# Fewer products for the size bounds, Strassen sums left in PSUM, and a small scaling on GpSimd

## The chip, the core and the metric

The kernel runs on one core of a Trainium2 chip. The metric is the device time of one execution in microseconds (us). The engines are TensorE (PE, with its weight loads listed as PEld), VectorE (DVE), ScalarE (ACT), GpSimd (POOL) and SyncE (SP), which only issues DMAs here. Each engine runs its own queue in order and waits for others by semaphores.

## The reference

Two attention layers over 2048 tokens, model width 1024, 32 heads of 32, written side by side in the output.

```
A: q, k, v = x@wq, x@wk, x@wv        # 4 segments of 512 tokens
   per segment s: a_dot = softmax(q k^T/sqrt(32) + mask) v
                  a_mem = phi(q) M / (phi(q) z + 1e-6)
                  o     = g*a_mem + (1-g)*a_dot;  M += phi(k)^T v;  z += sum phi(k)
   out_A = o @ wo
B: q, k, v = split(x @ wqkv);  pq = q@w_phi, pk = k@w_phi     # per head
   phi(t) = [softmax(t), softmax(-t)]
   o = phi(pq) (phi(pk)^T v) / (phi(pq) sum(phi(pk)) + 1e-6)
   out_B = o @ wo
```

## The kernel before

Every large product is computed in fp16 with each operand split into a high and a low half, so that one product is three matmuls. For the split, values are scaled by a bound of their size; the bounds are computed on the chip.

The work is described as operations with an engine, a duration, a priority, and the buffers read and written. A planner (`Graph.run`) then lays all of them in one order per engine by list scheduling with these durations, takes PSUM banks (8, by kinds `proj`, `s`, `misc`, `pv`, `kv`) as they come free in the plan, and keeps operations that are marked `port` on DVE apart from those of POOL. The code order therefore sets only priorities; a changed operation can change the order of everything after it.

*Layer A* (to about 900 us) is 32 units: for each half of the sequence (two segments), eight groups of four heads, two segments each. `produce` makes the queries, keys and values of a unit, `attend` the attention. Before a unit, `bounds(k, segs)` makes scale factors for queries and keys of group `k`, and `bounds_v(k, segs)` those for values. A bound is a sum over partitions of (column maxima of the segment, `xam`) times (column sums of the weights, `wgb`, `wvb`): the kernel multiplies them on PE, with one segment's `xam` column broadcast as the 128x128 fp32 weights and the group's `wgb` columns as the moving operand, one product for each segment and each group. Then DVE scales and inverts (tile `bd`, `bv`), and POOL makes the remaining factors. The weights of the groups for the second half (`k >= 8`, for values `k >= 4`) are the same ones as for the first half, loaded again.

*Layer B* (from about 870 us) takes 8 pairs of token blocks. A product of 256 tokens by all 1024 columns is done by `strassen`: seven products of 12 matmuls each, in three PSUM banks X, Y, Z, with results `(row half, column half)`. Some products serve two results: `keep` (ACT) copies a bank to an SBUF tile of tag `cs` (`pk` for the first value products), and `add` (DVE) adds another bank to it. Product 4 ends in X, is added to the kept one, and product 6 goes on accumulating in X. Each result goes to `out`: for values `vout` (split on ACT and DVE); for keys and queries `expo`, which on DVE takes the maximum and the minimum over each head's 32 columns (`mx`), subtracts (tile `e`), has ACT take exponentials, sums them on DVE (`r`), for keys scales `r` by 1/EUP, and inverts it. POOL then multiplies `e` by `r`. The keys and values of all pairs come first (about 950 to 1250 us), with their sum products in bank kind `kv`; then the queries with the output projection (to about 1600 us); last, the output product of layer A.

Of the kernel before, what the change touches and what calls it, by code (L numbers as in the profile page):

```python
# [255 lines left out]
def tile_kernel(ctx: ExitStack, tc: tile.TileContext, ax, aw, awv, awo, beta, bx, bwqk, bwv, bphi, bwo, out):  # L256
# [51 lines left out]
    big = const.tile([128, 6], F32, name="big")  # L308
    nc.vector.memset(big, 0.0)
    wsc = const.tile([128, 3, 2, 2], F32, name="wsc")  # L310
    osc2 = const.tile([128, 2, 2], F32, name="osc2")
# [257 lines left out]
    def strassen(x, w, prio, kinds, tag, out):  # L569
# [15 lines left out]

        def add(t, ps):
            op(DVE, 0.62, lambda: nc.vector.tensor_tensor(t(), t(), ps(), op=OP.add), r=[ps], w=[t], prio=prio)  # L587
# [91 lines left out]
    def bounds(k, segs, prio):  # L679


        bd = bds.get(k) or bds.setdefault(k, G.buf("a", [128, 5, 2, 2], F32, "bd", 4))
        s0, n, kk = segs[0], len(segs), k % NG
        v, w = slice(s0 % 2, s0 % 2 + n), [(bd, x % 2) for x in segs]
        ps = bank("misc", [128, 2, 2], "bounds")
        for x in segs:
            op(PE, 0.14, lambda x=x: nc.tensor.matmul(
                ps()[:, x % 2], xam[:, x:x + 1].to_broadcast([128, 128]), wgb[:, kk], start=True, stop=True),
               r=[(xams, x), (wgbs, (kk, 0)), (wgbs, (kk, 1))], w=[ps], prio=prio, need=[bd])
        op(DVE, 0.1, lambda: nc.vector.tensor_scalar(bd()[:, 3, v], ps()[:, v], 2.0 ** -12, 1e-30, op0=OP.mult, op1=OP.max),  # L690
           r=[ps], w=w, prio=prio)
        op(DVE, 0.12, lambda: nc.vector.reciprocal(bd()[:, 2, v], bd()[:, 3, v]), w=w, prio=prio)
        op(DVE, 0.1, lambda: nc.vector.scalar_tensor_tensor(
            bd()[:, 4, v, 0], bd()[:, 3, v, 0], SCALE, bd()[:, 3, v, 1], op0=OP.mult, op1=OP.mult), w=w, prio=prio)
        op(POOL, 0.2, lambda: nc.gpsimd.tensor_tensor(
            bd()[:, 0, v], xsc[:, s0:s0 + n, 0:1].to_broadcast([128, n, 2]), wgs[:, kk, :, 0][:, None, :].to_broadcast([128, n, 2]), op=OP.mult),
           r=[*((xscs, x) for x in segs), (wgss, (kk, 0)), (wgss, (kk, 1))], w=w, prio=prio)
        op(POOL, 0.2, lambda: nc.gpsimd.tensor_tensor(bd()[:, 2, v], bd()[:, 2, v], bd()[:, 0, v], op=OP.mult), w=w, prio=prio)
        op(POOL, 0.2, lambda: nc.gpsimd.tensor_scalar(bd()[:, 1, v], bd()[:, 0, v], -1.0, None, op0=OP.mult), w=w, prio=prio)

    def bounds_v(k, segs, prio):

        bv = bvs.get(k) or bvs.setdefault(k, G.buf("a", [128, 3, 2], F32, "bv", 3))
        s0, n, kk = segs[0], len(segs), k % 4
        v, w = slice(s0 % 2, s0 % 2 + n), [(bv, x % 2) for x in segs]
        ps = bank("misc", [128, 2], "bounds")
        for x in segs:
            op(PE, 0.14, lambda x=x: nc.tensor.matmul(
                ps()[:, x % 2:x % 2 + 1], xam[:, x:x + 1].to_broadcast([128, 128]), wvb[:, kk:kk + 1], start=True, stop=True),
               r=[(xams, x), (wvbs, kk)], w=[ps], prio=prio, need=[bv])  # L710
# [3 lines left out]
        a, b = s0 % 2, (s0 + n - 1) % 2  # L714
        op(DVE, 0.1, lambda: nc.vector.scalar_tensor_tensor(
            big[:, 0:1], bv()[:, 1, a:a + 1], bv()[:, 1, b:b + 1], big[:, 0:1], op0=OP.max, op1=OP.max), r=w, w=[(bigs, 0)], prio=prio)
        op(POOL, 0.4, lambda: nc.gpsimd.tensor_scalar(bv()[:, 0, v], xsc[:, s0:s0 + n, 0], wvs[:, kk, 0:1], None, op0=OP.mult),
           r=[*((xscs, x) for x in segs), (wvss, kk)], w=w, prio=prio)

    def values(u):  # L720

        s, g = units[u]
        k = group(u) // 2
        w, x, P, d = wt[k, "v"], xt[s], 2 * u, un[u]
        d["bv"] = bv = bvs[k]
        i2, n0, vf = s % 2, 128 * (g % 2), vfb[u % 3]
        sc = d["sc"] = G.buf("a", [128, 4], F32, "sc", 4)
        op(POOL, 0.39, lambda: nc.gpsimd.tensor_scalar(sc(), gate1[:, 4 * g:4 * g + 4], bv()[:, 1, i2:i2 + 1], None, op0=OP.mult),
           r=[gates, (bv, i2)], w=[sc], prio=P + VPRIO)
# [5 lines left out]
        op(ACT, 0.62, lambda: nc.scalar.activation(vf()[:, :, 0:128], ps(), AF.Copy, scale=bv()[:, 0, i2:i2 + 1]),  # L735
           r=[ps, (bv, i2)], w=[vf], prio=P + VPRIO)

    def produce(u):
# [10 lines left out]
        for m in (1, 0):  # L749
            ps = bank("proj", [128, 512])  # L750
            product((ps, ps), lambda a, c: (w, (m, a, c // 4), lambda m=m: w()[:, m, a, c, :]), at(x), NC, P, dur=0.215)
            E = P
            op(ACT, 0.57, lambda ps=ps, m=m: nc.scalar.activation(half(m, 0), ps(), AF.Copy, scale=bd()[:, 2, i2, m:m + 1]),
               r=[ps, (bd, i2)], w=[(h3, (m, 0))], prio=E)
            op(DVE, 0.6, lambda ps=ps, m=m: nc.vector.scalar_tensor_tensor(
                half(m, 1), ps(), bd()[:, 2, i2, m:m + 1], half(m, 0), op0=OP.mult, op1=OP.subtract),
               r=[ps, (h3, (m, 0)), (bd, i2)], w=[(h3, (m, 1))], prio=E)
# [4 lines left out]
            if (m == 1 and s < NSEG - 1) or (m == 0 and s > 0):  # L762
                d[name] = p = G.buf("a", [128, 512], F32, name, 2)
                z = G.buf("a", [128, 512], F32, "z", 1)
                for o, i in ((z, 0), (p, 1)):
                    op(ACT, 0.59, lambda o=o, i=i, ps=ps, m=m: nc.scalar.activation(o(), ps(), AF.Relu, scale=bd()[:, i, i2, m:m + 1]),
                       r=[ps, (bd, i2)], w=[o], prio=E)
# [4 lines left out]
    def attend(u):  # L772
        s, g = units[u]
        d, P = un.pop(u), 2 * u + 1
        st, vl, vf, bd, bv, i2 = stk[u % 3], vlb[u % 2], vfb[u % 3], bds[group(u)], d["bv"], s % 2
        KR, QR = [(st, (1, r)) for r in range(3)], [(st, (0, r)) for r in range(3)]
# [60 lines left out]
        def v4(t):  # L837
            return t()[:, :, 0:128].rearrange("p c (h d) -> p c h d", d=32)

        act(0.52, lambda: nc.scalar.activation(vl()[:, :, :, 33:65], v4(vf), AF.Copy, scale=bv()[:, 2, i2:i2 + 1]),  # L840
            r=[vf, (bv, i2)], w=[(vl, 0)])
        dve(0.6, lambda: nc.vector.scalar_tensor_tensor(
            vl()[:, :, :, 0:32], v4(vf), bv()[:, 2, i2:i2 + 1], vl()[:, :, :, 33:65], op0=OP.mult, op1=OP.subtract),
            r=[vf, (bv, i2), (vl, 0)], w=[(vl, 1)], port=True)
# [46 lines left out]
        def scores(blocks, diag):  # L891
# [13 lines left out]
            pe(0.218, f, r=KR + QR + [(st, (1, 3))] + [(st, (0, 3 + h)) for h, _ in blocks], w=[ps])  # L905
            act(0.59, lambda: nc.scalar.activation(ps(), ps(), AF.Exp, bias=0.0, scale=bd()[:, 4, i2, 0:1]), r=[(bd, i2)], w=[ps])  # L906
            ph = G.buf("a", [128, 2, 512], F16, "ph", 6)
# [234 lines left out]
    for u in range(NU):  # L1142
# [12 lines left out]
        if u % 4 == 1 and u // 4 + 1 < 8:  # L1155
            load_wv(u // 4 + 1, 2 * u + 0.5)
            if u // 4 + 1 < 4:
                keep_wv(u // 4 + 1)
            x = 2 * ((u // 4 + 1) // 4)
            bounds_v(u // 4 + 1, [x, x + 1], 2 * u + 0.5)  # L1160
        if u % 2 and k < NG:
            keep_wg(k, [(un[u]["h3"], (1, 1))])
        if u % 2 == 0 and k + 2 < NU // 2:
            load_wg(k + 2, 2 * u + 3.5)
            x = 2 * ((k + 2) // NG)
            bounds(k + 2, [x, x + 1], 2 * u + 3.5)
        attend(u)
# [11 lines left out]
    def expo(ps, prio, sk, up=None):  # L1179
# [23 lines left out]
        if up is not None:  # L1203
            op(DVE, 0.1, lambda: nc.vector.tensor_scalar(r(), r(), 1.0 / up, None, op0=OP.mult), r=[r], w=[r], prio=prio)
        op(DVE, 0.27, lambda: nc.vector.reciprocal(r(), r()), r=[r], w=[r], prio=prio)  # L1205
# [345 lines left out]
    for c in range(NT // 2):  # L1551
# [12 lines left out]
        def half(t, h):  # L1564
            return lambda: t()[:, h]
# [96 lines left out]
```

## Time and profile before

| | |
|---|---|
| median of 3 runs | 1764.49 us (1764.32 to 1765.12) |
| the profiled execution | 1767.9 us, span 1766.2 us |
| granted PE clock, mean over the span | 0.990 |
| PE busy | 1714.1 us (97%) |
| DVE busy | 1430.7 us (81%) |
| ACT busy | 1147.8 us (65%) |
| POOL busy | 978.2 us (55%) |

A row of the groups reads: line, engine, operation, output<-inputs, shape, count | busy us, mean ns of one | idle time of the engine just before them and who ended it. In the listing in order of time a row starts with the start and the length in us. Matmuls overlap in the pipeline, so the busy time of a single matmul is longer than the distance to the next; a gap in PE's busy time is a real gap. A fp32 matmul shows as two rows of PE.

### The profile page before, as it was taken

How to read it: one execution, taken by the hardware profiler on the slowest of the kernel's cores; microseconds unless marked ns; L12 is line 12 of the kernel's file. 1: busy time of each engine (PE TensorE's matmuls, PEld its weight loads, DVE VectorE, ACT ScalarE, POOL GpSimd, SP SyncE). 2: the span in 40 equal slices, each digit the busy share in tenths (PEclk: the TensorE clock that was granted, in tenths of full speed). 3: DMA queues.
4: the chain of work that ended last, by engine and by line, in shares of the span. 5: the costliest groups of instructions: out<-in, count | busy, mean ns of one | idle time of the engine just before them, and what ended most of it. 6: DMA issues, size and time to landing. Idle time of an engine off the chain costs nothing.

```text
span 1766.2 us, 39229 instructions
## 1 busy us (share of the span) xinstructions
PE 1714.1 (97%) x14722; PEld 1040.3 (59%) x14722; DVE 1430.7 (81%) x3330; ACT 1147.8 (65%) x2115; POOL 978.2 (55%) x1191
## 2 busy tenths in 40 slices
PE   7999998999999999999999998999999999999999
PEld 5766666767766776776754444544455555554444
DVE  6988998899998887889765999788998888886541
ACT  6878888888787888686863665666444454344431
POOL 6336567654579897756641767545566665430000
PEclk9999999999999999999999999999999999999999
DMA  6545456665665654754556453469213332234311
GB/s 206 178 142 157 133 183 208 199 207 170 215 199 160 182 160 106 228 166 134 172 163 234 168 174 107 144 194 356 102 60 96 109 108 88 63 140 135 120 66 66
DMA packets 194143, 273.64 MB, mean 155 GB/s; under 512 B 72224, under 2 KB 125216, under 8 KB 187424
## 3 DMA queue, kind: packets, MB, share of 16 engines
q1 hardware_dynamic: 193952, 271.13, 48.4%
q8 instruction: 116, 1.90, 0.5%
q14 instruction: 75, 0.61, 0.1%
HBM read 160.12 MB, written 85.00 MB: 139 GB/s over the span
## 4 chain that ended last, share of the span: by engine, by line
PE 52%; DVE 17%; ACT 4%; issue 1%; DMA 1%; POOL 0%; ACTq 0%; DVEq 0%; POOLq 0%
PE proj L369 12%; PE proj L577 11%; PE misc L369 8%; PE proj L1590 5%; PE s L1590 2%; DVE mx L1192 2%; PE s L902 2%; DVE e L1196 2%; PE s L801 2%; PE pv L938 2%; DVE r L1202 2%; DVE e L1194 1%; ACT e L1199 1%; PE misc L1590 1%; PE pv L1536 1%
## 5 line engine op out<-in xcount | busy, mean ns | idle before, releaser
L369 PE MATMUL proj<-S,S 128*128 128x128 f16 (+1 forms) x3072 | 500.9, 299 | 5.6 <-ACT S L396 3.6
L369 PEld LDWEIGHTS <-S 128*128 128x128 f16 x4608 | 331.0, 98 | 154.6 <-issue 9.1
L577 PE MATMUL proj<-S,S 128*128 128x512 f16 x1584 | 368.8, 384 | 11.3 <-DVE cs L587 5.9
L577 PEld LDWEIGHTS <-S 128*128 128x128 f16 x2016 | 193.9, 99 | 234.3 <-issue 20.8
L915 POOL TENSOR_SCALAR_AFFINE_SELECT ph<-ph 128x256 f16<-128x256 f16 (+1 forms) x448 | 194.1, 455 | 158.7 <-DVE ph L909 134.5
L909 DVE SCALAR_TENSOR_TENSOR ph<-s,ph 128x512 f16<-128x512 f32 x320 | 210.1, 683 | 55.6 <-ACT ph L908 53.1
L807 DVE CUSTOM_DVE_ANT_0 s<-s,causal 128x512 f32<-128x512 f32 (+3 forms) x512 | 242.1, 510 | 13.0 <-PE s L801 9.3
L906 ACT ACTIVATE s<-s,bd 128x512 f32<-128x512 f32 x320 | 212.7, 713 | 23.5 <-PE s L902 21.1
L908 ACT ACTIVATE ph<-s 128x512 f16<-128x512 f32 x320 | 191.5, 658 | 0.8 <-PE pv L938 0.2
L369 PE MATMUL misc<-S,ot 128*128 128x512 f16 x768 | 175.3, 381 | 0.0
L1199 ACT ACTIVATE e<-e,sk 128x256 f32<-128x256 f32 x256 | 113.3, 497 | 83.8 <-DVE e L1196 79.2
L369 PEld LDWEIGHTS <-ot 128*128 128x128 f16 x768 | 73.8, 98 | 82.0 <-issue 1.3
L1504 POOL TENSOR_TENSOR e<-e,zb 128x512 f32<-128x512 f32 x64 | 82.0, 1305 | 70.5 <-DVE r L1202 50.0
L902 PE MATMUL s<-S 104*128 104x512 f16 (+3 forms) x512 | 113.0, 299 | 5.5 <-DVE ph L909 3.3
L801 PE MATMUL s<-S 96*128 96x512 f16 (+3 forms) x512 | 113.7, 300 | 2.3 <-DVE ph L909 1.5
L1308 POOL TENSOR_TENSOR e<-e,r 128x1024 f32<-128x1024 f32 x32 | 66.2, 2081 | 76.6 <-DVE r L1205 60.6
L369 PE MATMUL proj<-wv,S 128*128 128x128 f16 x1536 | 103.2, 220 | 0.1
L938 PEld LDWEIGHTS <-ph 128*128 128x128 f16 x2560 | 87.6, 96 | 18.3 <-issue 3.4
L1202 DVE TENSOR_REDUCE r<-e 128x32 f32<-128x1024 f32 x64 | 76.8, 1210 | 25.5 <-ACT e L1199 25.4
L938 PE MATMUL pv<-vl,ph 128*128 128x66 f16 (+1 forms) x2560 | 92.1, 185 | 2.3 <-DVE oall L942 0.9
L1517 POOL TENSOR_TENSOR e<-e,r 128x1024 f32<-128x1024 f32 x32 | 62.3, 1950 | 37.7 <-DVE r L1515 36.4
L807 DVE DVE_READ_ACCUMULATOR2_ANT mt<- 128x1 f32 x512 | 72.3, 141 | 0.0
(305 smaller groups left out, 3369.1 us busy)
## 6 DMA issues: line engine op xcount, KB each, us to landing
S<-xf_d SPq DMA_DIRECT2D x126, 256.0 KB
S<-h SPq DMA_DIRECT2D x192, 128.0 KB
S<-wf_d SPq DMA_DIRECT2D x21, 1024.0 KB
st<-bwqk SPq DMA_DIRECT2D x64, 256.0 KB
out<-os SPq DMA_DIRECT2D x40, 256.0 KB
S<-aw SPq DMA_DIRECT2D x16, 512.0 KB
wa_d<-S SPq DMA_DIRECT2D x16, 512.0 KB
wf_d<-fo SPq DMA_DIRECT2D x32, 256.0 KB
```

The costliest lines, as they stand in the source:

```text
L369: op(PE, dur, lambda c=c, a=a, b=b, lv=lv, rv=rv: nc.tensor.matmul(pv(), lv(), rv(), start=(c == 0 and a + b == 0), stop=(c == n - 1 and a ...
L577: op(PE, 0.215, lambda n=n, a=a, b=b, lv=lv, rv=rv: nc.tensor.matmul(ps(), lv(), rv(), start=(start and n == 0 and a + b == 0), stop=(n == ...
L801: nc.tensor.matmul(ps()[:, o:o + 128 * i + 128], st()[0:96, 0, h, 128 * i:128 * i + 128], st()[0:96, 1, h, 0:128 * i + 128], start=True, s ...
L807: dve(0.12 + 0.00113 * n, lambda h=h, i=i, o=o, n=n: nc.vector.tensor_tensor_reduce(ps()[:, o:o + n], ps()[:, o:o + n], causal[:, 512 - n: ...
L902: nc.tensor.matmul(ps()[:, o:o + n], st()[0:104, 1, h, 128 * j:128 * j + 128], st()[0:104, 0, h, 128 * j:512], start=True, stop=True)
L906: act(0.59, lambda: nc.scalar.activation(ps(), ps(), AF.Exp, bias=0.0, scale=bd()[:, 4, i2, 0:1]), r=[(bd, i2)], w=[ps])
L908: act(0.5, lambda: nc.scalar.activation(ph()[:, 0], ps(), AF.Copy, scale=2.0 ** 14), r=[ps], w=[(ph, 0)])
L909: dve(0.6, lambda: nc.vector.scalar_tensor_tensor(ph()[:, 1], ps(), 2.0 ** 14, ph()[:, 0], op0=OP.mult, op1=OP.subtract), r=[ps, (ph, 0)], ...
L915: nc.gpsimd.affine_select(pd, pd, pattern=[[0, n], [1, 128]], compare_op=OP.is_ge, fill=0.0, base=0, channel_multiplier=-1)
L938: nc.tensor.matmul(ps()[:, i, n0:n1], ph()[:, a, o:o + 128], vl()[:, j, h, n0:n1], start=(i == 0 and a == 0), stop=(j == min(i, 2)), skip_ ...
L1199: op(ACT, 0.41, lambda i=i: nc.scalar.activation(e()[:, 4 * i:4 * i + 4], e()[:, 4 * i:4 * i + 4], AF.Exp, bias=0.0, scale=sk()[:, i:i + 1 ...
L1590: op(PE, 0.215, lambda n=n, a=a, b=b: nc.tensor.matmul(ps(), v(a)[:, n, :], wform[w]()[:, b, n, :], start=(start and n == 0 and a + b == 0 ...
```

## The change

1. *Bounds.* In the first half of layer A, where two segments are bounded together, POOL multiplies `xam` by `wgb` (tile `pr`) and one PE product with a column of ones as weights sums over the partitions for both segments. For the second half, all eight groups (for values all four) are done at once at the first call: one product for each segment with all groups' columns, one chain on DVE and POOL, in one tile (tag `os`, and `bvh`). PE has 4 + 6 + 2 products for `bounds` and 2 + 3 + 2 for `bounds_v`, where it had 32 and 16; DVE has 29 small instructions fewer in them.
2. *Strassen.* `add` gets a target. Result (0, 0) is written over bank Y, result (0, 1) over bank Z, and their readers take them from PSUM; result (1, 1) stays in SBUF. The reader's flag `port` follows.
3. *expo.* The scaling of `r` by 1/EUP goes from DVE to POOL.

```diff
@@ strassen
-        def add(t, ps):
-            op(DVE, 0.62, lambda: nc.vector.tensor_tensor(t(), t(), ps(), op=OP.add), r=[ps], w=[t], prio=prio)
+        def add(t, ps, o):
+            op(DVE, 0.62, lambda: nc.vector.tensor_tensor(o(), t(), ps(), op=OP.add), r=[t, ps], w=[o], prio=prio)
...
-        add(p1, Y)
-        out(0, 0, p1)
+        add(p1, Y, Y)
+        out(0, 0, Y)
...
-        add(p5, X)
+        add(p5, X, p5)
         out(1, 1, p5)
         mult(Z, 5)
-        add(u2, Z)
-        out(0, 1, u2)
+        add(u2, Z, Z)
+        out(0, 1, Z)
@@ bounds (bounds_v likewise, with wvb, and a maximum over all groups into big)
-        for x in segs:
-            op(PE, 0.14, lambda x=x: nc.tensor.matmul(
-                ps()[:, x % 2], xam[:, x:x + 1].to_broadcast([128, 128]), wgb[:, kk], start=True, stop=True),
...
+        if n > 1 and not rest:
+            pr = G.buf("a", [128, 2, nk, 2], F32, "pr", 1)
+            op(POOL, 0.2, lambda: nc.gpsimd.tensor_tensor(
+                pr(), xam[:, s0:s0 + n, None, None].to_broadcast(shape), wgb[:, None, ks].to_broadcast(shape), op=OP.mult),
+               r=[(xams, x) for x in segs] + wg, w=[pr], prio=prio)
+            op(PE, 0.14, lambda: nc.tensor.matmul(ps(), one.to_broadcast([128, 128]), pr(), start=True, stop=True),
+               r=[pr], w=[ps], prio=prio, need=[bd])
+        else:
+            for x in segs:
+                op(PE, 0.14, lambda x=x: nc.tensor.matmul(
+                    ps()[:, x % 2], xam[:, x:x + 1].to_broadcast([128, 128]), wgb[:, ks], start=True, stop=True),
+                   r=[(xams, x)] + wg, w=[ps], prio=prio, need=[bd])
@@ the loop over units
-            bounds_v(u // 4 + 1, [x, x + 1], 2 * u + 0.5)
+            if u // 4 + 1 <= 4:
...
-            bounds(k + 2, [x, x + 1], 2 * u + 3.5)
+            if k + 2 <= NG:
@@ expo
-            op(DVE, 0.1, lambda: nc.vector.tensor_scalar(r(), r(), 1.0 / up, None, op0=OP.mult), r=[r], w=[r], prio=prio)
+            op(POOL, 0.15, lambda: nc.gpsimd.tensor_scalar(r(), r(), 1.0 / up, None, op0=OP.mult), r=[r], w=[r], prio=prio)
```

In the changed kernel, lines of `strassen` stand 1 further down, and those of `expo` 41 (L1192, L1194, L1196, L1202, L1205 are L1233, L1235, L1237, L1243, L1246); POOL's multiplication L1308 is L1349.

From about 50 us on the order of every engine is laid anew. Three places show what the parts do.

PE in the second half of layer A, before the change: two bounds' products for keys and queries (L687) and two for values (L708) between score matmuls (L801).

```order
L801 MATMUL s<-S_149 128x256
L687 MATMUL misc<-wgb,xam 128x2 x2
L708 MATMUL misc<-wvb,xam 128x1 x2
L801 LDWEIGHTS S_149
L801 MATMUL s<-S_149 128x512
```

PE after the change, earlier, at the first call for the second half (L742 for values, L704 for keys and queries, among score and projection matmuls).

```order
L370 LDWEIGHTS S_6351
L370 MATMUL proj<-S_823,S_6351 128x512
L742 MATMUL misc<-wvb,xam 128x4
L704 MATMUL misc<-wgb,xam 128x16
L370 LDWEIGHTS S_6351
L370 MATMUL proj<-S_823,S_6351 128x512
```

One product now has the columns of all groups of a segment, and no product of the bounds follows after these in PE's order.

DVE in the key stage of layer B, before: the sums go to `cs`, and `r` is summed (L1202), scaled (L1204) and inverted (L1205) on DVE.

```order
L1202 TENSOR_REDUCE r<-e 128x32
L1204 TENSOR_SCALAR r<-r 128x32
L1205 RECIPROCAL r<-r 128x32
L1194 TENSOR_TENSOR e<-cs,mx 128x16x32
L1196 TENSOR_TENSOR e<-mx,cs 128x16x32
L1194 TENSOR_TENSOR e<-cs,mx 128x16x32
L1196 TENSOR_TENSOR e<-mx,cs 128x16x32
L1192 TENSOR_REDUCE mx<-proj 128x16 x2
L1194 TENSOR_TENSOR e<-proj,mx 128x16x32
L1196 TENSOR_TENSOR e<-mx,proj 128x16x32
```

DVE in the same stage after the change (L588 is the Strassen sum).

```order
L588 TENSOR_TENSOR s<-cs,s 128x512
L1233 TENSOR_REDUCE mx<-s 128x16 x2
L1246 RECIPROCAL r<-r 128x32
L1235 TENSOR_TENSOR e<-s,mx 128x16x32
L1243 TENSOR_REDUCE r<-e 128x32
L1237 TENSOR_TENSOR e<-mx,s 128x16x32
L1233 TENSOR_REDUCE mx<-proj 128x16 x2
L1235 TENSOR_TENSOR e<-proj,mx 128x16x32
L1246 RECIPROCAL r<-r 128x32
L1237 TENSOR_TENSOR e<-mx,proj 128x16x32
```

The sum, the maxima and the subtractions now have a PSUM bank as operand, and the scaling is gone from between the sum of `r` and its reciprocal. In the whole order 5 of the 32 reciprocals stand directly behind their own sum, and 9 more have one instruction between.

POOL in the key stage before: the multiplications by `r` (L1308), the splits of the result (L1343) and those of later token blocks (L1120).

```order
L1120 TENSOR_TENSOR kls<-zb,kls 128x512 x2
L1308 TENSOR_TENSOR e<-e,r 128x1024 x2
L1343 TENSOR_TENSOR pt<-e,pt 128x512
L1308 TENSOR_TENSOR e<-e,r 128x1024 x2
L1175 TENSOR_SCALAR sk<-swf,pst 128x4 x2
```

POOL in the same stage after the change, with the scaling as L1245.

```order
L1159 TENSOR_TENSOR kls<-zb,kls 128x512 x3
L1349 TENSOR_TENSOR e<-e,r 128x1024
L1245 TENSOR_SCALAR r<-r 128x32 x2
L1384 TENSOR_TENSOR pt<-e,pt 128x512
L1349 TENSOR_TENSOR e<-e,r 128x1024 x2
L1245 TENSOR_SCALAR r<-r 128x32
```

The scalings stand among operations of 512 and 1024 columns; ten of the 32 come right behind a multiplication L1349.

More of the change, by code (lines that the diff above doesn't have):

```diff
@@ L624, in tile_kernel @@
     bigs, swfs, wscs, oscs, phss = (G.fixed(t) for t in (big, swf, wsc, osc2, phs))
-    pstb, wmb, topb = (G.fixed(t) for t in (pst, wm, tops))
+    pstb, wmb, topb, vmxs = (G.fixed(t) for t in (pst, wm, tops, vmx))
     osc = G.fixed(oa_d)
@@ L690, in bounds @@
-        op(DVE, 0.1, lambda: nc.vector.tensor_scalar(bd()[:, 3, v], ps()[:, v], 2.0 ** -12, 1e-30, op0=OP.mult, op1=OP.max),
+        rest = k >= NG
+        ks = slice(0, NG) if rest else slice(k % NG, k % NG + 1)
+        nk = NG if rest else 1
+        if k not in bds:
+            t = G.buf(*(("stage", [128, 4, 2, nk, 2], F32, "os", 1) if rest else ("a", [128, 4, 2, nk, 2], F32, "bd", 4)))
+            for i in range(nk):
+                bds[k + i] = (t, lambda i=i: t()[:, :, :, i, :])
+        bd = bds[k][0]
@@ new lines, in bounds @@
+        s0, n = segs[0], len(segs)
+        v, w, shape = slice(s0 % 2, s0 % 2 + n), [(bd, x % 2) for x in segs], [128, n, nk, 2]
+        ps = bank("misc", [128, 2, nk, 2], "bounds")
+        wg = [(wgbs, (i, m)) for i in range(ks.start, ks.stop) for m in range(2)]
+        if n > 1 and not rest:
[10 more added lines that the diff above has]
+                   r=[(xams, x)] + wg, w=[ps], prio=prio, need=[bd])
@@ L701, in bounds_v @@
     def bounds_v(k, segs, prio):
[L703 to L710, printed above, removed]
+        rest = k >= 4
+        ks = slice(0, 4) if rest else slice(k % 4, k % 4 + 1)
+        nk = 4 if rest else 1
+        if k not in bvs:
+            t = G.buf("a", [128, 3, 2, nk], F32, "bvh" if rest else "bv", 1 if rest else 2)
+            for i in range(nk):
+                bvs[k + i] = (t, lambda i=i: t()[:, :, :, i])
+        bv = bvs[k][0]
+        s0, n = segs[0], len(segs)
+        v, w, shape = slice(s0 % 2, s0 % 2 + n), [(bv, x % 2) for x in segs], [128, n, nk]
+        ps = bank("misc", [128, 2, nk], "bounds")
+        wv = [(wvbs, i) for i in range(ks.start, ks.stop)]
+        if n > 1 and not rest:
+            pr = G.buf("a", [128, 2, nk, 1], F32, "pr", 1)
+            op(POOL, 0.2, lambda: nc.gpsimd.tensor_tensor(
+                pr()[:, :, :, 0], xam[:, s0:s0 + n, None].to_broadcast(shape), wvb[:, None, ks].to_broadcast(shape), op=OP.mult),
+               r=[(xams, x) for x in segs] + wv, w=[pr], prio=prio)
+            op(PE, 0.14, lambda: nc.tensor.matmul(ps(), one.to_broadcast([128, 128]), pr()[:, :, :, 0], start=True, stop=True),
+               r=[pr], w=[ps], prio=prio, need=[bv])
+        else:
+            for x in segs:
+                op(PE, 0.14, lambda x=x: nc.tensor.matmul(
+                    ps()[:, x % 2], xam[:, x:x + 1].to_broadcast([128, 128]), wvb[:, ks], start=True, stop=True),
+                   r=[(xams, x)] + wv, w=[ps], prio=prio, need=[bv])
         op(DVE, 0.1, lambda: nc.vector.tensor_scalar(bv()[:, 1, v], ps()[:, v], 2.0 ** -15, 1e-30, op0=OP.mult, op1=OP.max),
@@ L713, in bounds_v @@
         op(DVE, 0.12, lambda: nc.vector.reciprocal(bv()[:, 2, v], bv()[:, 1, v]), w=w, prio=prio)
[L714 to L718, printed above, removed]
+        if rest:
+            op(DVE, 0.1, lambda: nc.vector.tensor_reduce(vmx, bv()[:, 1, v], axis=AX.XY, op=OP.max), r=w, w=[vmxs], prio=prio)
+            op(DVE, 0.1, lambda: nc.vector.tensor_tensor(big[:, 0:1], big[:, 0:1], vmx, op=OP.max), r=[vmxs], w=[(bigs, 0)], prio=prio)
+        else:
+            a, b = s0 % 2, (s0 + n - 1) % 2
+            op(DVE, 0.1, lambda: nc.vector.scalar_tensor_tensor(
+                big[:, 0:1], bv()[:, 1, a], bv()[:, 1, b], big[:, 0:1], op0=OP.max, op1=OP.max), r=w, w=[(bigs, 0)], prio=prio)
+        op(POOL, 0.4, lambda: nc.gpsimd.tensor_tensor(
+            bv()[:, 0, v], xsc[:, s0:s0 + n, 0][:, :, None].to_broadcast(shape), wvs[:, ks, 0][:, None].to_broadcast(shape), op=OP.mult),
+           r=[*((xscs, x) for x in segs), *((wvss, i) for i in range(ks.start, ks.stop))], w=w, prio=prio)
     def values(u):
@@ L765, in produce @@
                 for o, i in ((z, 0), (p, 1)):
[L766 removed]
+                    op(ACT, 0.59, lambda o=o, i=i, ps=ps, m=m: nc.scalar.activation(o(), ps(), AF.Relu, scale=bdv()[:, i, i2, m:m + 1]),
                        r=[ps, (bd, i2)], w=[o], prio=E)
@@ L1164, in tile_kernel @@
             load_wg(k + 2, 2 * u + 3.5)
-            x = 2 * ((k + 2) // NG)
-            bounds(k + 2, [x, x + 1], 2 * u + 3.5)
+            if k + 2 <= NG:
+                x = 2 * ((k + 2) // NG)
+                bounds(k + 2, [x, x + 1], 2 * u + 3.5)
         attend(u)
```

39 lines of the change are left out of this document (19 added, 20 removed).

## The prediction

> **What bounds the kernel now.** I read the page's busy times and chain first, then busy time stage by stage, then who PE waits for in the stage where it is short, and last the instructions around one such wait.
>
> ```profile
> PE 1714.1 (97%) x14722; PEld 1040.3 (59%) x14722; DVE 1430.7 (81%) x3330; ACT 1147.8 (65%) x2115; POOL 978.2 (55%) x1191
> PE 52%; DVE 17%; ACT 4%; issue 1%; DMA 1%; POOL 0%; ACTq 0%; DVEq 0%; POOLq 0%
> ...
> 60.00:400.00 340.00, 327.21 (x3509) 232.52 (x3506) 301.81 (x848) 288.86 (x522) 203.18 (x309) 0.99 0.57 175
> 400.00:870.00 470.00, 469.08 (x5198) 334.52 (x5196) 407.77 (x1179) 374.32 (x680) 342.61 (x511) 1.00 0.57 170
> 870.00:950.00 80.00, 77.19 (x577) 42.32 (x574) 49.42 (x126) 42.15 (x73) 26.95 (x47) 0.98 0.66 212
> 950.00:1250.00 300.00, 285.59 (x1928) 142.08 (x1927) 262.40 (x426) 183.61 (x378) 176.23 (x131) 0.98 0.56 191
> 1250.00:1350.00 100.00, 94.11 (x679) 50.20 (x679) 95.31 (x172) 46.57 (x95) 59.70 (x44) 1.00 0.20 61
> 1350.00:1550.00 200.00, 199.97 (x1332) 102.88 (x1330) 159.34 (x276) 90.23 (x172) 117.04 (x89) 1.00 0.30 95
> ```
>
> The stage rows give length, then busy time of PE, PEld, DVE, ACT and POOL, then the granted clock. PE is the bound, and there are two kinds of stage. From 400 to 870 (attention) and from 1350 to 1550 (queries of the linear attention) PE is never idle: only less work for PE helps there. From 950 to 1250 (keys and values of the linear attention) PE is unbusy for 300 − 285.6 = 14.4 us and runs at 0.98, another 0.02 × 300 = 6 us: 20.4 us are lost, while DVE is 87% busy. Between 60 and 400 the loss is 12.8 us plus 3.4 of clock.
>
> For 950 to 1250, first PE's waits, then the engines around the longest one:
>
> ```profile
> PE proj L577 <- ACT cs L583: 5.3, 3, 2.8
> PE proj L577 <- DVE cs L587: 4.4, 2, 4.2
> PE kv L1350 <- DVE pt L1343: 4.2, 6, 1.6
> ...
> 1088.80 3.92 DVE L1232 SCALAR_TENSOR_TENSOR ot<-cs,pst,ot 128x512 f16<-128x512 f32 x2
> 1089.81 4.68 POOL L1308 TENSOR_TENSOR e<-e,r 128x1024 f32<-128x1024 f32 x2
> 1092.64 2.40 DVE L1194 TENSOR_TENSOR e<-cs,mx 128x512 f32<-128x512 f32 x1
> 1094.96 1.64 DVE L1196 TENSOR_TENSOR e<-mx,cs 128x512 f32<-128x512 f32 x1
> 1099.51 0.68 DVE L587 TENSOR_TENSOR cs<-cs,proj 128x512 f32<-128x512 f32 x1
> 1100.24 2.29 PE L577 MATMUL proj<-S,S 128*128 128x512 f16 x5 [4.21 <-DVE cs L587]
> ...
> 1624.83 2.59 PE s L1590 x12
> ```
>
> Nearly all of the 14.4 us (5.3 + 4.4 + 4.2) are waits behind DVE's queue or behind ACT copies that share it. The longest shows how: while POOL runs its multiplications (L1308), DVE's instructions that take `cs` from SBUF are drawn out to 2.40 and 1.64 us; the third sum of the Strassen product (L587) sits behind them, and product 6, which writes the bank that this sum reads, starts 4.2 us late. The last row is from the chain in order of time, further on: 12 such matmuls in a row take 2.59 us.
>
> **The change, part by part.** How long DVE takes from either memory in this stage:
>
> ```profile
> L1192 DVE TENSOR_REDUCE mx<-cs 128x16 f32<-128x512 f32 x50 | 32.3, 672 | 0.4
> L1196 DVE TENSOR_TENSOR e<-mx,cs 128x512 f32<-128x512 f32 x25 | 30.9, 1237 | 0.0
> L1194 DVE TENSOR_TENSOR e<-cs,mx 128x512 f32<-128x512 f32 x25 | 23.5, 940 | 0.0
> L1232 DVE SCALAR_TENSOR_TENSOR ot<-cs,pst,ot 128x512 f16<-128x512 f32 x15 | 20.2, 1357 | 0.0
> L1204 DVE TENSOR_SCALAR r<-r 128x32 f32<-128x32 f32 x32 | 11.9, 375 | 0.2
> L1192 DVE TENSOR_REDUCE mx<-proj 128x16 f32<-128x512 f32 x16 | 10.4, 674 | 0.0
> L1196 DVE TENSOR_TENSOR e<-mx,proj 128x512 f32<-128x512 f32 x8 | 5.4, 676 | 0.0
> L1194 DVE TENSOR_TENSOR e<-proj,mx 128x512 f32<-128x512 f32 x8 | 5.4, 676 | 0.0
> L1232 DVE SCALAR_TENSOR_TENSOR ot<-proj,pst,ot 128x512 f16<-128x512 f32 x5 | 3.7, 734 | 3.6 <-ACT ot L1230 3.6
> ```
>
> *Sums in PSUM.* Each Strassen product has four results: one was already read from PSUM, two more now are, and one stays in `cs`. Of the 24 or so subtractions of each kind that read `cs` here, two of three (16) move: 16 × (1.237 − 0.676) = 9.0 us at L1196, 16 × (0.940 − 0.676) = 4.2 at L1194. Of the 15 value splits, 10 move: 10 × (1.357 − 0.734) = 6.2. The reductions cost the same (672 and 674 ns). The sum itself only changes its target; L587 with 0.68 us stands for it, since a write from DVE into PSUM of this form is not in the trace. Together DVE is relieved of 19.4 us. In the query stage the same move saves DVE time that PE does not wait for (199.97 of 200 busy): nothing; between 1250 and 1350 I count nothing either. The banks are held longer, by the sum's readers, about four DVE instructions of 0.68 us; a Strassen product is 84 matmuls, 7 × 2.59 = 18 us, and the next one wants those banks only after its own first products, so this costs nothing while DVE's lag stays under about 10 us.
>
> [...]
>
> *The scaling of r on POOL.* It removes 32 × 0.375 = 11.9 us from DVE. On POOL the nearest rows are these, and its neighbours in the queue stand with them:
>
> ```profile
> L699 POOL TENSOR_SCALAR bd<-bd 128x4 f32<-128x4 f32 x14 | 3.1, 220 | 0.0
> L959 POOL TENSOR_TENSOR rd<-rd,sc 128x16 f32<-128x16 f32 x30 | 8.2, 274 | 8.2 <-DVE rd L958 8.2
> L1308 POOL TENSOR_TENSOR e<-e,r 128x1024 f32<-128x1024 f32 x32 | 66.2, 2081 | 76.6 <-DVE r L1205 60.6 <-DVE r L1204 15.8
> ...
> 1101.16 0.34 DVE L1205 RECIPROCAL r<-r 128x32 f32<-128x32 f32 x1
> 1101.58 1.91 POOL L1308 TENSOR_TENSOR e<-e,r 128x1024 f32<-128x1024 f32 x1 [0.87 <-DVE r L1205]
> ```
>
> So some 0.28 us each (between 0.22 for 4 columns and a little above 0.27 for 16), 9 us of POOL, which is idle 124 of the 300. But the step between two DVE instructions now crosses to another queue and back, and DVE's reciprocal waits in order with all that stands behind it. In the new order 5 of the 32 reciprocals follow their own sum directly: with two handoffs of 0.08 us or a little more (DVE ends at 1101.50, POOL starts at 1101.58) at least 0.46 us each, 2.3 us. Ten scalings stand on POOL right behind a multiplication L1308 of 2.08 us; if half of it is still to run, that is 10 × 1.04 = 10.4 us. I take 13 us of new DVE waits; the ends are 2 us and, if all 32 wait for a whole L1308 and the scaling, 32 × 2.4 = 76.
>
> Net, DVE gains 19.4 + 11.9 − 13 = 18 us of 262. What PE gets back of its 20.4 us cannot be read off; the ends are all of it, and a loss if the waits exceed the 31 us removed. I take half, **10 us**, since over half of the DVE relief survives and all three waits stand behind DVE.
>
> *Bounds.* On PE, one place, and the count:
>
> ```profile
> 613.05 0.50 PE L369 MATMUL proj<-S,S 128*128 128x128 f16 x6
> 613.39 0.56 PE L687 MATMUL misc<-wgb,xam 128*128 128x2 f32 x4
> 613.81 1.02 PE L369 MATMUL proj<-S,S 128*128 128x512 f16 x4
> ...
> L687 PE MATMUL misc<-wgb,xam x64: 166/251/251, 16.4 to 766.2; 128*128 128x2 f32 x64
> L708 PE MATMUL misc<-wvb,xam x32: 167/250/271, 27.8 to 722.5; 128*128 128x1 f32 x32
> ```
>
> An fp32 product is two rows, so there are 32 + 16 = 48, and a pair holds PE for 613.81 − 613.39 = 0.42 us: 0.21 each. After the change there are 19. Twenty of the 29 removed are those of the second half of the units (16 + 8 become 2 + 2), after 400 us, where PE is never idle: 20 × 0.21 = **4.2 us**. The other nine lie before 400, worth 1.9 us, but there nine multiplications on POOL (0.22 each by L699) now stand ahead of the product, and PE waits in order if POOL is late: between 1.9 us of gain and 9 × 1.2 (one POOL operation of 128x512 in front) = 11 of loss. I take nothing, since PE's products are placed after other matmuls and this stage has idle time already. DVE loses 29 small instructions here, all under PE: nothing.
>
> Sum: 4.2 + 10 + 0 = 14.2 us. The profiled execution took 1767.9 us (span 1766.2), which gives 1753.7; it was 3.4 us above the median 1764.5, so the median becomes **1750 us** (−0.8%). About 0.2% (3.5 us) is what a measurement of this kernel tells from no change.
>
> **Rivals.**
> *A. The key stage gives nothing.* L1343 on DVE (two SBUF inputs, not touched) and the third sum keep PE waiting, and the new waits take the rest. Only the bounds remain: 1764.5 − 4.2 = 1760.
> *B. Slower: DVE waits for POOL.* The place is the reciprocal behind the scaling in the key stage. It decides when the mean wait of the 32 passes 31.3 / 32 = 1.0 us, half of an L1308. At 1.6 us, DVE has 20 us more to do than before, and the stage, with 37 us of DVE idle time that are partly waits themselves, passes about half to PE: 1764.5 − 4.2 + 10 = 1770. For it: ten scalings right behind L1308, and each queue's lag now passes to the other. Against: POOL is only 59% busy. [...]
> *C. A new order, new gaps.* From 50 us on the whole order is laid anew. The stage 870 to 950 shows what one late piece costs: 2.8 us unbusy and 0.02 × 80 = 1.6 of clock. Three such places more, in the attention or at a change of stage, make 13 us: about 1764, no change.
> *D. The stall goes wholly*, and with it some of the 5.9 us unbusy between 1250 and 1350: 1764.5 − 4.2 − 20.4 − 2 = 1738.
>
> **How the numbers follow.** Forecast 50% (1742 to 1757), A 20%, B 14%, C 10%, D 6%. Faster by over 0.2% (under 1761): the forecast, D and two thirds of A, 0.50 + 0.06 + 0.13 = 0.69; within 0.2%: the rest of A and most of C, 0.15; slower: B and some of C, 0.16. The range 1737 to 1768 takes in D, the forecast, A and C and leaves out most of B.
>
> **What would show it.** *Bounds:* rows of two matmuls per pair gone after 400 us, and the stage of the same work about 4 us shorter with PE still full. *Sums:* L1194 and L1196 (L1235 and L1237 now) from `proj`, `misc` and `s` near 676 ns, the sum into PSUM near 0.68 us. *Scaling:* its POOL row near 0.28 us, and DVE idle before the reciprocal of some 13 us in all, put down to POOL. *Key stage:* PE's waits for `cs` under half of 9.7 us. I am wrong if DVE's idle time before the reciprocal exceeds 31 us (B), if the waits for `cs` stay (A), or if PE is short where it was full (C).

## The result, and the profile after

The changed kernel takes 1740.2 us (median of 4 runs, 1739.29 to 1741.96) against 1764.8 for the kernel before on the same chip: ratio 0.9855, 95% interval 0.9834 to 0.9876. The profiled execution has a span of 1737.6 us against 1766.2. A second series with the same order gave 1738.65 and 0.9833 (0.9819 to 0.9846). The kernel before has two levels, near 1764 and near 1769 us (last section), so ratios are taken within one series and single executions are compared by stage.

The forecast was 1750 in 1737 to 1768, faster with 0.69: the sign and the places were right, the gain was 24.6 us between the medians (29.5 by the ratio of the second series, 0.0167 of 1769) where 14.5 were forecast. The time lies in the range, but below the 1742 to 1757 of the forecast itself, beside rival D's 1738.

The page after (busy times, chain), then busy time by stage: PE, PEld, DVE, ACT, POOL, granted clock, and the share and rate of the DMAs. The stages are cut at three events: first Strassen matmul (865.3), first and last sum product of the keys (952.4, 1221.5).

```profile
PE 1696.4 (98%) x14664; PEld 1029.2 (59%) x14664; DVE 1382.1 (80%) x3269; ACT 1146.2 (66%) x2115; POOL 976.0 (56%) x1208
PE 68%; DVE 18%; ACT 9%; POOL 2%; issue 2%; DMA 1%; POOLq 0%; ACTq 0%; DVEq 0%; SPq 0%
...
60.00:400.00 340.00, 332.93 (x3606) 236.14 (x3604) 309.95 (x870) 298.08 (x537) 209.73 (x330) 1.00 0.59 179
400.00:865.30 465.30, 461.07 (x5150) 329.81 (x5149) 398.90 (x1165) 366.63 (x669) 334.10 (x482) 1.00 0.58 171
865.30:952.40 87.10, 86.34 (x570) 43.68 (x568) 53.09 (x108) 45.01 (x81) 27.73 (x46) 1.00 0.64 216
952.40:1221.50 269.10, 260.63 (x1871) 132.46 (x1870) 222.30 (x385) 179.54 (x370) 176.75 (x161) 0.99 0.59 204
```

The kernel before, cut at the same three events:

```profile
400.00:875.20 475.20, 474.29 (x5276) 339.48 (x5274) 412.90 (x1199) 374.92 (x681) 344.54 (x513) 1.00 0.57 169
875.20:967.80 92.60, 89.80 (x585) 45.71 (x583) 56.14 (x125) 47.38 (x84) 28.58 (x46) 0.98 0.64 210
967.80:1255.10 287.30, 271.57 (x1894) 136.54 (x1895) 254.73 (x413) 179.77 (x370) 174.79 (x130) 0.98 0.55 189
```

Of the 28.6 us between the two executions, 9.9 come up to the first Strassen matmul (875.2 to 865.3), 5.5 in the first value products (92.6 to 87.1) and 18.2 between the first and the last sum product of the keys (287.3 to 269.1, with DVE 32 us less busy). After that, the new kernel takes 516.1 us to the end of its span, the old one 511.1: 5.0 more, in part work moved there, since the key stage has 23 rows of PE fewer. In the first value products the old kernel has one long wait of PE, for a tile of layer A that POOL makes; the new order has it no more:

```profile
PE misc L970 <- POOL osum L965: 2.8, 1, 2.8
```

The key stage after: the groups of DVE that answer to those shown of before (L1237 and L1235 were L1196 and L1194, L1233 was L1192), the scaling on POOL, and who PE and DVE's reciprocal wait for.

```profile
L1237 DVE TENSOR_TENSOR e<-mx,cs 128x512 f32<-128x512 f32 x7 | 8.7, 1247 | 0.0
L1235 DVE TENSOR_TENSOR e<-cs,mx 128x512 f32<-128x512 f32 x7 | 6.6, 948 | 0.0
L1237 DVE TENSOR_TENSOR e<-mx,s 128x512 f32<-128x512 f32 x7 | 4.7, 675 | 0.0
L1235 DVE TENSOR_TENSOR e<-misc,mx 128x512 f32<-128x512 f32 x7 | 4.7, 678 | 0.0
L588 DVE TENSOR_TENSOR s<-cs,s 128x512 f32<-128x512 f32 x12 | 8.2, 687 | 4.4 <-PE s L578 4.4
L1233 DVE TENSOR_REDUCE mx<-cs 128x16 f32<-128x512 f32 x16 | 10.3, 676 | 0.2
L1233 DVE TENSOR_REDUCE mx<-misc 128x16 f32<-128x512 f32 x14 | 9.3, 682 | 0.1
...
L1245 POOL TENSOR_SCALAR r<-r 128x32 f32<-128x32 f32 x31 | 9.8, 317 | 37.0 <-DVE r L1243 33.3 <-DVE wsc L383 3.5 <-DVE tops L498 0.2
...
PE kv L1391 <- ACT pt L1381: 4.5, 1, 4.5
PE kv L1391 <- DVE pt L1384: 2.0, 3, 0.8
PE proj L578 <- ACT cs L584: 1.7, 2, 1.0
...
DVE r L1246 <- POOL r L1245: 3.4, 6, 1.4
```

Only 7 subtractions of each kind still read `cs`, and they are as drawn out as before; the others take what PSUM reads took before. PE's waits for the kept copies and the third sum, 9.7 us before, are 1.7. POOL waits for DVE at the scaling (33.3 us), hardly DVE for POOL (3.4).

Is it SBUF itself that is slow, or SBUF beside POOL? The kernel before tells. Its subtractions over the whole span, with the shortest, the median and the longest in ns:

```profile
L1194 DVE TENSOR_TENSOR e<-cs,mx x48: 621/682/2397, 955.8 to 1566.2; 128x512 f32<-128x512 f32 x48
L1194 DVE TENSOR_TENSOR e<-proj,mx x16: 672/675/680, 971.7 to 1567.9; 128x512 f32<-128x512 f32 x16
L1196 DVE TENSOR_TENSOR e<-mx,cs x48: 627/684/2395, 956.4 to 1570.3; 128x512 f32<-128x512 f32 x48
L1196 DVE TENSOR_TENSOR e<-mx,proj x16: 669/674/683, 972.3 to 1568.5; 128x512 f32<-128x512 f32 x16
```

The median read from SBUF is as quick as one from PSUM. Of the 94 from SBUF that start between 950 and 1560 us, 53 ran while no POOL instruction did, and took 0.68 us in the mean; the 41 others overlap one, and took 1.05 (L1194) and 1.45 us (L1196). The 30 from PSUM took 0.68 us with POOL and without.

### The profile page after: what moved, and what is told of

It reads as the page before. It is cut to its first block, busy times and chain, and to the rows that moved or that the text cites. A ratio compares the mean times of both kernels' runs of the same rounds, so it can differ in the third digit from the quotient of the medians.

```text
span 1737.6 us, 39086 instructions
## 1 busy us (share of the span) xinstructions
PE 1696.4 (98%) x14664; PEld 1029.2 (59%) x14664; DVE 1382.1 (80%) x3269; ACT 1146.2 (66%) x2115; POOL 976.0 (56%) x1208
## 4 chain that ended last, share of the span: by engine, by line
PE 68%; DVE 18%; ACT 9%; POOL 2%; issue 2%; DMA 1%; POOLq 0%; ACTq 0%; DVEq 0%; SPq 0%
PE proj L370 20%; PE proj L578 14%; PE misc L370 7%; PE proj L1631 5%; PE s L840 3%; DVE s L846 3%; PE s L941 3%; PE pv L977 2%; PE s L1631 2%; PE s L578 2%; ACT s L945 2%; ACT ph L947 2%; DVE ph L948 2%; DVE mx L1233 2%; PE misc L1631 1%
## 5 line engine op out<-in xcount | busy, mean ns | idle before, releaser
L578 PE MATMUL proj<-S,S 128*128 128x512 f16 x1584 | 361.4, 380 | 2.4 <-ACT cs L584 2.4
L954 POOL TENSOR_SCALAR_AFFINE_SELECT ph<-ph 128x256 f16<-128x256 f16 (+1 forms) x448 | 190.0, 447 | 149.7 <-DVE ph L948 115.9
L846 DVE CUSTOM_DVE_ANT_0 s<-s,causal 128x256 f32<-128x256 f32 (+3 forms) x512 | 242.3, 509 | 12.5 <-PE s L840 9.3
L948 DVE SCALAR_TENSOR_TENSOR ph<-s,ph 128x512 f16<-128x512 f32 x320 | 209.5, 684 | 52.1 <-ACT ph L947 51.1
L945 ACT ACTIVATE s<-s,os 128x512 f32<-128x512 f32 x160 | 106.8, 725 | 7.7 <-PE s L941 7.7
L945 ACT ACTIVATE s<-s,bd 128x512 f32<-128x512 f32 x160 | 104.7, 699 | 6.9 <-PE s L941 6.4
L1243 DVE TENSOR_REDUCE r<-e 128x32 f32<-128x1024 f32 x64 | 77.3, 1210 | 20.8 <-ACT e L1240 20.7
L1558 POOL TENSOR_TENSOR e<-e,r 128x1024 f32<-128x1024 f32 x32 | 61.9, 1938 | 40.4 <-DVE r L1556 31.6
```

The lines of the kernel that those rows point to most:

```text
L578: op(PE, 0.215, lambda n=n, a=a, b=b, lv=lv, rv=rv: nc.tensor.matmul(ps(), lv(), rv(), start=(start and n == 0 and a + b == 0), stop=(n == ...
L846: dve(0.12 + 0.00113 * n, lambda h=h, i=i, o=o, n=n: nc.vector.tensor_tensor_reduce(ps()[:, o:o + n], ps()[:, o:o + n], causal[:, 512 - n: ...
L948: dve(0.6, lambda: nc.vector.scalar_tensor_tensor(ph()[:, 1], ps(), 2.0 ** 14, ph()[:, 0], op0=OP.mult, op1=OP.subtract), r=[ps, (ph, 0)], ...
L954: nc.gpsimd.affine_select(pd, pd, pattern=[[0, n], [1, 128]], compare_op=OP.is_ge, fill=0.0, base=0, channel_multiplier=-1)
```

## The experiments

*One part alone, the order planned anew each time.*

```diff
e1_bounds:   the changed kernel with the old targets of the sums and the scaling on DVE
e2_sums:     the kernel before with   add(p1, Y, Y); out(0, 0, Y)   and   add(u2, Z, Z); out(0, 1, Z)
e3_scale:    the kernel before with   op(POOL, 0.15, ... nc.gpsimd.tensor_scalar(r(), r(), 1.0 / up ...
e4_no_scale: the changed kernel with  op(DVE, 0.1, ... nc.vector.tensor_scalar(r(), r(), 1.0 / up ...
```

> The bounds alone (sums in SBUF, scaling on DVE). Theory: 29 fp32 products fewer take about 6 us of work off PE, so 4 to 7 us faster than before; the key stage keeps its waits for the Strassen sums (about 10 us) and its half-clock stretches. Rival (the new order is the cause): the stalls at about 270, 905 and 1594 us go or come with any new order, so this one lands anywhere from 12 us faster to 5 us slower, and PE's work does not explain the difference.

> The two Strassen sums in PSUM alone. Theory: this is where most of the time came from: the drawn-out subtractions go to 676 ns, PE's waits for the kept copies and the third sum in the key stage fall from 9.7 us to under 4, 12 to 17 us faster than before. Rival (the scaling is what frees DVE): under 6 us. Layer A is the same order as before up to its end, so any difference lies after about 870 us.

> The scaling of r on POOL alone. Theory: it takes 12 us off DVE in the key stage but leaves the drawn-out subtractions; 0 to 6 us faster. Rival (the scaling is what frees DVE): 10 us or more. Rival (DVE waits for POOL): slower, with over 10 us of DVE idle before the reciprocal.

> The whole change without the scaling (it stays on DVE). Theory: 18 to 24 us faster than before, 1 to 6 us slower than the whole change. Rival (the scaling is what frees DVE): 10 us or more slower than the whole change. Rival (the new order is the cause): any place between.

| kernel | median, us | ratio to before (95%) |
|---|---|---|
| bounds alone | 1763.26 | 0.9983 (0.9971 to 0.9995) |
| sums alone | 1758.17 | 0.9952 (0.9934 to 0.9970) |
| scaling alone | 1759.46 | 0.9948 (0.9931 to 0.9964) |
| all but the scaling | 1752.53 | 0.9923 (0.9895 to 0.9950) |

In us of 1769, the three single parts are 3, 8.5 and 9, together 20.7, less than the whole change's 25.6 to 29.5. Every theory missed somewhere: the bounds brought half of what was expected, the sums less, the scaling more than its own theory allowed, and the kernel without the scaling lost some 13 us against the whole. The bounds alone reach the first Strassen matmul 10.7 us before the old kernel (864.5 against 875.2), but of this lead 6.2 us are left at the end of the two profiled executions. Since each of these kernels was planned anew, they mix a part with an order. So the order was fixed next.

*One part taken back or added, the order kept.* The sequence in which the planner had laid the operations was written out as a table and followed:

```diff
-            t, e = min((max(free[e], min(map(start, l))), e) for e, l in lists.items() if l)
...
+            t, o, e = min(((rank[x.prio[1]], i, x, e) for e, l in lists.items() for i, x in enumerate(l) if start(x) < never),
+                          key=lambda y: y[0])[1:]
+            t = max(free[e], start(o))
```

> The changed kernel with its own order of every engine written out as a table, and only the target of the two sums put back to SBUF, so that nothing differs but where 48 sums stand. Theory (DVE's SBUF reads beside POOL cost the time): the subtractions from SBUF are drawn out again to 900 to 1250 ns, PE waits in the key stage for the kept copies and the third sum, 8 to 15 us slower than the whole change. Rival (the new order brought it): within 3 us of the whole change.

> The changed kernel with its own order as a table, and only the scaling of r put back on DVE at the same place. Theory (the scaling takes 12 us off DVE and almost no wait comes for it): 5 to 12 us slower than the whole change, with L1204's old mean near 375 ns. Rival (the 10 us between the kernel without the scaling and the whole one come from the order that the planner made): within 3 us of the whole change.

> The kernel before with its own order of every engine as a table, and only the two sums written over PSUM (a few matmuls of a following product stand later, where its bank is still read). Nothing else differs, so layer A cannot change. Theory (DVE's SBUF reads beside POOL cost the time): the key stage alone becomes 8 to 14 us shorter, 0.5 to 0.8% faster than before. Rival (the gain needs the new order): under 0.2% faster, because the order keeps DVE's instructions where they were late.

> The changed kernel again, its own order written out as a table: the same instructions in the same order, as the measure for its neighbours. Every theory: the ratio to before as it was, 0.9855 within 0.002.

| kernel | median, us | ratio to before (95%) |
|---|---|---|
| the change's order, unchanged | 1738.65 | 0.9833 (0.9819 to 0.9846) |
| the change's order, sums in SBUF | 1761.41 | 0.9959 (0.9945 to 0.9972) |
| the change's order, scaling on DVE | 1744.60 | 0.9865 (0.9852 to 0.9879) |
| before's order, sums in PSUM | 1759.56 | 0.9949 (0.9935 to 0.9964) |

The second and third row ran in one series, the first and the last in another, so a difference between the two series is known to some 3 us. The change's order as a table is 0.0022 from the 0.9855 above, where 0.002 was expected; the kernel before took 1769 us in this series.

Busy time by stage again (length, then PE busy), in this order: what followed the key stage in the kernel before; before's order with sums in PSUM, the key stage and what follows it; the change's order with sums in SBUF, the value products and the key stage; the change's order with the scaling on DVE.

```profile
1255.10:1375.00 119.90, 115.30 (x772) 59.40 (x769) 109.05 (x196) 54.51 (x109) 75.29 (x57) 1.00 0.23 71
...
973.10:1242.00 268.90, 263.29 (x1893) 134.36 (x1893) 231.51 (x413) 179.36 (x371) 164.61 (x130) 1.00 0.60 202
1242.00:1362.00 120.00, 110.62 (x732) 57.40 (x729) 103.03 (x188) 51.07 (x101) 69.33 (x53) 0.96 0.20 62
...
866.80:961.30 94.50, 89.12 (x568) 44.30 (x565) 54.89 (x108) 45.30 (x81) 28.58 (x46) 0.96 0.58 197
961.30:1242.60 281.30, 265.25 (x1870) 133.69 (x1869) 239.71 (x385) 180.98 (x370) 185.69 (x161) 0.98 0.57 195
...
953.10:1227.70 274.60, 262.62 (x1871) 132.87 (x1870) 233.00 (x416) 179.78 (x370) 168.19 (x130) 0.99 0.58 200
```

With before's order and nothing but the targets of the sums changed (and a few matmuls set later, whose bank is still being read), the key stage falls from 287.3 to 268.9 us (1893 and 1894 rows of PE, so the same work): 18.4 us, as much as the whole change shows there, and more than the 8 to 14 expected. PE's idle time falls by 10.1 us of these (15.7 to 5.6); most of the rest goes with the granted clock, 0.98 before and 1.00 now. The stage behind it has lost clock (0.96) and PE time (9.4 us unbusy against 4.6), which gives part of it back: over all executions 9.0 us are left (0.0051 of 1769). The other way round, SBUF targets in the change's order cost 281.3 − 269.1 = 12.2 us in the key stage and 94.5 − 87.1 = 7.4 in the value products, and 22.3 in total (0.0126), where 8 to 15 were expected. The 7.4 us are not a drawn-out read: there PE waits 5.2 us for ACT's copy into the kept tile, and the clock is 0.96.

```profile
PE proj L784 <- ACT pk L790: 5.2, 2, 4.7
```

Two such tiles exist there, and with the sum in SBUF a kept tile is in use until its readers are through; with the sum in PSUM it is free after the addition. No run parts this effect from the slower reads. It also belongs to the change's order, which was planned with the early release: in before's order the value products take 92.6 us with sums in SBUF and in PSUM alike, with the same wait for POOL's `osum` and none for a kept tile.

```profile
PE misc L1178 <- POOL osum L1173: 2.8, 1, 2.8
880.50:973.10 92.60, 89.80 (x585) 45.20 (x583) 56.02 (x125) 47.27 (x84) 27.71 (x46) 0.98 0.64 210
```

So the 5.5 us that the change gains in this stage came with its order. The scaling back on DVE costs 5.5 us of the key stage (274.6) and 5.7 of the total (0.0032 of 1769). The other 8 us or so by which the kernel without the scaling was slower (1752.5 against 1744.6) come from the order that the planner made for it.

*What the bounds' products cost PE, and what an order is worth.*

```diff
e5_pad:   - nc.tensor.matmul(ps(), one..., pr(), start=True, stop=True)
          + [nc.tensor.matmul(ps(), one..., pr(), start=True, stop=True) for _ in range(2)]   # 8 and 4 times in the second half
e6_relay: - op(PE, 0.14, ... xam[:, x:x + 1] ... wgb[:, kk] ...       # kernel before
          + op(PE, 0.2,  ... xam[:, x:x + 1] ... wgb[:, kk] ...
```

> The whole change with the bounds' products issued several times over (2 times in the first half, 8 and 4 times in the second), so that PE again has 48 of them, in the same order and with the same results. Theory (fp32 products take PE's own time): 0.21 us for each of 29, 6 us slower than the whole change. Rival (what the bounds brought is a luckier order in layer A): within 2 us of the whole change.

> The kernel before with one number of the planner changed: a bounds' product is planned as 0.2 us instead of 0.14. Not one instruction is added or taken away, but from 50 us on the order is another. Theory (parts, not order): within 4 us of before. Rival (order is worth as much as the parts): 5 us or more to either side, with other half-clock stretches in layer A.

The padded kernel takes 1746.21 us, ratio 0.9874 (0.9861 to 0.9888): 0.0041 × 1769 = 7.3 us more than the change in the other series, and its first Strassen matmul comes at 872.4 instead of 865.3.

```profile
400.00:872.40 472.40, 468.17 (x5220) 335.47 (x5220) 402.92 (x1171) 369.81 (x672) 336.44 (x483) 1.00 0.58 170
```

Not all of these 7.1 us need be the products'. First the last place with padding, in the padded kernel and then in the changed one; then both between 210 and 230 us:

```profile
415.71 0.95 PE L742 MATMUL misc<-wvb,xam 128*128 128x4 f32 x8
416.52 1.94 PE L704 MATMUL misc<-wgb,xam 128*128 128x16 f32 x16
418.31 0.59 PE L370 MATMUL proj<-S,S 128*128 128x512 f16 x2
...
410.94 0.28 PE L742 MATMUL misc<-wvb,xam 128*128 128x4 f32 x2
411.07 0.37 PE L704 MATMUL misc<-wgb,xam 128*128 128x16 f32 x2
411.30 0.59 PE L370 MATMUL proj<-S,S 128*128 128x512 f16 x2
...
210.00:230.00 20.00, 17.93 (x229) 14.36 (x227) 16.56 (x55) 18.46 (x36) 13.91 (x21) 0.83 0.63 210
210.00:230.00 20.00, 17.21 (x238) 13.72 (x237) 18.28 (x57) 19.95 (x38) 14.29 (x21) 1.00 0.68 223
```

Ten products more make 2.60 − 0.36 = 2.24 us here, 0.22 each. Ten others of the second half stand at 386 and 405 us, so at this price all 20 make 4.5 us. The other 2.6 us are those of the nine products of the first half together with a stretch at half clock near 220 us that the changed kernel's profiled execution does not have; how much of them is the nine products' is not shown. The sums show best that a part has no price apart from its order: taken back from the change's order they cost 22.3 us in total, put into before's order they bring 9.0.

The kernel with another planned number, without one instruction changed, takes 1768.01 us, 0.9992 (0.9983 to 1.0001): in total this other order is worth nothing that the interval shows, though its first Strassen matmul comes at 883.4 us instead of 875.2 (880 in other executions of before's order).

*Going further.*

```diff
e8_three:      -        add(p5, X, p5)
               -        out(1, 1, p5)
               +        add(p5, X, Y)
               +        out(1, 1, Y)
g4_three_late: the same, and for ACT's scaling of layer A's output weights
               -               r=[(wscs, (2, 0))], ...
               +               r=[(wscs, (2, 0)), zb], ...
```

> The whole change, and the third Strassen sum also in PSUM: the sum over product 4 is written to bank Y, which its first reader has left by then. Theory (DVE's SBUF reads beside POOL cost the time): the last subtractions from SBUF, 7 of each kind at 1250 and 950 ns in the key stage, go to 676 ns, 6 us less on DVE and 2 to 5 us faster than the whole change. Rival (PE has little left to win there, bank Y is now held longer): within 2 us either way.

> As the one with three sums in PSUM, and the scaling of layer A's output weights on ACT waits until the sums over the keys have been copied. Theory: the one long wait left in the key stage, 4.5 us of PE for ACT's copy of the keys behind those scalings, goes with its half-clock stretch, 4 to 8 us faster than the changed kernel. Rival (ACT waits for the exponentials' input there anyway): within 2 us of the kernel with three sums.

Three sums in PSUM: 1741.91 us, 0.9848 (0.9834 to 0.9861), 2.7 us slower than the change's 0.9833 in the same series, if at all, where 2 to 5 us faster were expected. DVE did get lighter in the key stage (209.5 us busy against 222.3) and the stage shorter (264.6 against 269.1, with 14 fewer rows of PE in it), but PE had only 1.7 us of such waits left, and the stages before and after took more. With the weights' scaling held back: 1736.45 us, 0.9818 (0.9804 to 0.9831), the fastest kernel here, faster than the change by 0.0015, which the intervals do not separate, and less than the 4 to 8 us expected. The long wait that this edit was to remove is still there:

```profile
PE kv L1391 <- ACT pt L1381: 5.0, 1, 5.0
...
1208.23 0.91 ACT L1240 ACTIVATE e<-e,sk 128x256 f32<-128x256 f32 x2 [4.01 <-DVE e L1237]
```

ACT's copy of the keys stands behind exponentials that wait for DVE, as the rival had it; the weights' scalings were not the cause. The rival's size was wrong too: it allowed 2 us from the kernel with three sums, and 5.3 us (0.0030) were measured. What the edit gained came after the key stage; no run says how.

## Why the prediction was right or wrong

*Bounds.* Price per product right (0.21 forecast, 0.22 measured), and with it the 4.2 us for the 20 of the second half (4.5). The nothing for the nine products before 400 us may be too little, by 2.6 us at most in the padded kernel. POOL's multiplications `pr`, which I set against them, do not show among PE's waits. What the term left out is larger: layer A became 9.9 us shorter.

*Sums in PSUM.* The mechanism was right in each row: 675 to 678 ns from PSUM, 687 ns for the sum, and PE's waits for the kept copies and the third sum fell from 9.7 to 1.7 us. The same reduction took 676 ns from SBUF and 682 from PSUM. The step that failed is "half of 20.4 us": with the order kept, the sums alone gave 18.4 in the key stage. I had cut the gain for DVE waits that did not come. The nothing for the stage behind failed the other way: it gave back about half of the 18.4 in before's order, and the change is 5.0 us longer from there on.

*Scaling on POOL.* Its price was near (0.28 us forecast, 0.317 measured), the step that failed is the waits: 13 us of DVE were forecast, 3.4 came in the stage. POOL mostly waits for DVE there (33.3 us at this line), so it is ready when `r` comes, and the half multiplication that I charged to ten of them was rarely in the way. The part is worth 5.7 us in the same order, where my sum had about nothing left for it.

*Rivals.* D, the whole stall, came nearest with 1738, a rival given 6%. It has the key stage nearly right but not the rest: of the 15.4 us gained ahead of it (9.9 in layer A, 5.5 in the value products) its sum holds 4.2, and the 5.0 us lost behind it are not there. That the total came so near to D is luck in part. A and B did not happen. C happened on a small scale: a new wait of 4.5 us at the end of the key stage, and some of the 5.0 us more after it. The zero for the query stage held: PE was full in it before (199.97 of 200 us) and after (199.86 of the 200 from 1330 to 1530 us).

*Open.* Layer A is shorter by 9.9 us where the products explain 4.5 to 7.1. The kernels planned with the same bounds reach the first Strassen matmul between 864.5 and 866.8 us, so it is no accident of one execution. One place differs: before the change PE waits four times for DVE between 266 and 273 us, 0.5 to 1.5 us each, and the clock between 264 and 282 us is 0.81, where the new kernel has 1.00 from 60 us on to the first Strassen matmul.

```profile
264.00:282.00 18.00, 13.82 (x165) 10.87 (x164) 11.68 (x32) 18.00 (x35) 15.71 (x23) 0.81 0.66 197
```

Whether fewer products or the new order removed it, no run here settles.

## What to carry to other kernels

Where a queue is late because its instructions are drawn out while another engine runs, look at where the operands lie before looking at the amount of work: the same subtraction cost 0.68 us from PSUM, as much from SBUF alone, and 1.05 to 1.45 us from SBUF beside a GpSimd instruction, and that delay reached PE through DVE's queue (4.2 us at the third sum). A planner that lays everything anew mixes each edit with an order: write the order out as a table and change one thing in it, and read the stage in which it acts, since the next stage can give part back.

## What the runs showed of the hardware

The same instructions in the same order did not take the same time here. The kernel before, and three that share its order up to the linear attention, reached the first Strassen matmul at two times, near 875 and near 880 us. Here are its row and the clock between 200 and 300 us, of before, then of the kernel with the scaling alone:

```profile
L577 PE MATMUL proj<-S,S x1584: 376/379/634, 875.2 to 1560.4; 128*128 128x512 f16 x198
200.00:300.00 100.00, 93.23 (x957) 65.24 (x955) 86.20 (x240) 89.39 (x161) 69.64 (x95) 0.97 0.57 179
...
L577 PE MATMUL proj<-S,S x1584: 376/379/634, 880.0 to 1552.0; 128*128 128x512 f16 x198
200.00:300.00 100.00, 94.30 (x961) 67.80 (x959) 82.15 (x230) 87.85 (x158) 69.41 (x95) 0.91 0.55 173
```

A few short gaps of PE lie at this place, and the granted clock over these 100 us was 0.97 in one execution and 0.91 in the other; the sums alone repeated the first (875.9), before's order with sums in PSUM the second (880.5). The 4.8 us between them are about the distance of the two levels of the kernel before; that they are its cause is not shown, since the profiled execution took the earlier time and still needed 1767.9 us in all. The changed kernel's runs lie within 3 us in each series. In the clock's own records in the traces of the kernel before and of the changed kernel, the granted clock is 1.00 or 0.50. Before the change, three stretches at 0.50 last 6.8 us and five 3.4 us, the last of them at the end of the execution; after, one lasts 6.8 us, two 3.4, and one of 2.9 ends the execution. What sets the clock, no run here shows.
